# Rescheduling the prologue of a fused cosine-attention and MLP-mixer kernel: token MLPs spread one per slot, norms a slot ahead

## The chip, the cores and the metric

The kernel runs on one core of one Trainium2 chip. The metric is the device time of one execution in microseconds (us). Before the change it was 411.51 us, the median of 3 runs (410.36 to 411.86).

## The reference, cut to what matters

```python
# q, k, v: (8, 12, 448, 64) f32; w_tok1 (448, 256), w_tok2 (256, 448), w_ch1 (768, 1536), w_ch2 (1536, 768)
q_n, k_n = q / (norm(q) + 1e-6), k / (norm(k) + 1e-6)
attn = softmax(q_n @ k_n.T / tau)                    # tau = 0.1
x = (attn @ v) laid out as (8, 448, 768)
u = x + (relu(x.T @ w_tok1) @ w_tok2).T              # token MLP
out = u + relu(u @ w_ch1) @ w_ch2                    # channel MLP
```

## The kernel before

Work goes by pairs of heads: 8 batches of 6 pairs, 48 in all. A loop pass is called a *slot* here; slot `i` does the scores of pair `i`, the product with v of pair `i - 1`, and older pairs' token MLPs. The channel MLP is cut into units (one group of matmuls each) that wait in a list and are fed into the slots as filler for TensorE.

The helpers that the argument touches:

```python
def load_qk(i):                       # q and k of a pair, 224 KB each, on SyncE's DMA queue
    ...
    nc.sync.dma_start(out=st[nm][:]..., in_=src[b, h0:h0 + 2]...)
def square(i, a, act=False):          # squares of q or k: GpSimd, or ScalarE with act=True
def sums(i): nc.vector.tensor_reduce(...)            # row sums of the squares, VectorE
def norms(...):                       # 1/norm from the sums: ScalarE (and VectorE with dve=True)
def scale(i, a): (eng or nc.gpsimd).tensor_tensor(...)   # q, k times 1/norm, GpSimd
def cast_v(i): nc.gpsimd.tensor_copy(...)            # v to f16
def tpose(i): ...                     # q, k transposed by TensorE (pairs below 12), by DMA after
def tok1(i): ...                      # matmul and rectification on VectorE
def tok2(i, pe=False):
    ...
    nc.vector.tensor_tensor(out=u, in0=psU[:], in1=st["x"][:], op=ALU.add)
    if pe:
        return
    nc.sync.dma_start_transpose(out=ut[b][:, pj], in_=u.rearrange("p m d -> p (m d)"))
def upose(i): ...                     # the same transpose by TensorE, with a VectorE copy
def m_ch1(b, ct): ...                 # one channel unit: needs the transposed u of all six pairs
```

The slots of batch 0 (cut):

```python
for i in range(1, NP_ALL + 1):
    b, pj = i // NPAIR, i % NPAIR
    if i < NPAIR:
        toks = {2: [0], 3: [1], 4: [2], 5: [3, 4]}.get(i, [])
        ...                            # scores 0 and 1, sums and norms of pair i + 2 (i < 5)
        for t in toks[:1]: tok1(t)
        pv(i - 1, 0)
        ...
        for t in toks[:1]: tok2(t)     # ends in the DMA transpose of u
        pv(i - 1, 1)
        for t in toks[1:]: tok1(t)
        score(i, 3)
        ...
        for t in toks[1:]: tok2(t)
        if i == 1: place_w2()
        else: weights_ch1(i - 2)       # a quarter of w_ch1 (1.18 MB read) from GpSimd's queue
        load_v(i + 4)
        load_qk(i + 6)
        continue
    ...                                # slot 6: token MLP of pair 5, transposed by TensorE
    # slots 7 to 11: SC_AT, SQ_AT, SU_AT say which pairs are scaled, squared and summed;
    # feed(quota, 1.0) forces one channel unit at each of three places
```

## Time and profile before

| reading | value | view |
|---|---|---|
| TensorE, 90 us to the last matmul at 403.4 us | 100% busy but for 0.1 us | busy time by window |
| slots 2 to 4, 5, 6, 7, 8 to 11 | 14.4, 6.7, 7.0, 8.65, 28.1 us | same, by slot |
| TensorE idle in slots 2 to 11 | 10.9 us | same |
| clock at half | 18.8 to 22.2 and 83.7 to 87.1 us | same |
| DMA, 18 to 50 us | 201 GB/s | same |

Since TensorE has nothing but work from 90 us to its last matmul, all that can be gained lies in the first 90 us and in the 5.4 us after that matmul. The first view is busy time by window, for TensorE alone, with windows cut at the starts of the slots' first scores. The columns are length, TensorE's busy time (and instructions), granted clock (1.00 is full), share of the DMA engines, and GB/s moved. The DMA share adds up the times of packets, which overlap, so it can pass 1.

```profile
core 0: us, PE busy (x), PEclk, DMA share, GB/s
18.86:33.24 14.38, 12.79 (x193) 0.88 1.10 204
33.24:39.94 6.70, 5.00 (x83) 1.00 1.29 219
39.94:46.97 7.03, 4.45 (x70) 1.00 1.30 188
46.97:55.62 8.65, 7.22 (x84) 1.00 1.26 258
55.62:83.72 28.10, 24.49 (x304) 1.00 1.18 235
```

The rows are slots 2 to 4, 5, 6, 7 and 8 to 11. Length less busy time is idleness: 1.7 us in slot 5, 2.6 in slot 6, 1.4 in slot 7, 3.6 in slots 8 to 11. The second view lists what TensorE waited for from 12 to 100 us: engine, tile and line, then what released it, total us, times, longest. PE is TensorE, DVE VectorE, ACT ScalarE, POOL GpSimd, SPq SyncE's queue; L299 is a line of that kernel's file. Of the tiles, psS are scores and pt their exponentials; kq is q and k scaled, pst and qk the same transposed; psO is the product with v and x its result; psR, rt and psU are the token MLP's first product, its rectification and its second product; u is the sum with x, ut its transpose; psG is a channel unit; qf, kf and vf are loaded q, k and v, vt is v cast, sq the squares.

```profile
PE psU L299 <- DVE rt L288: 3.3, 4, 2.3
PE psS L256 <- ACT pt L258: 2.9, 5, 0.8
PE pst L235 <- POOL kq L221: 2.7, 3, 1.2
PE psG L321 <- DMA ut<-u: 1.4, 2, 1.3
```

The first line's 2.3 us falls in slot 11, where a rectification sits on VectorE behind a row sum whose squares GpSimd had not finished. The third view is SyncE's DMA queue as a timeline, which shows the order in which transposes and loads are issued:

```profile
37.69 8.13 SPq L305 DMA_TRANSPOSE ut<-u  x2
45.91 0.53 SPq L110 DMA_DIRECT2D vf<-in_v_dram  x1
46.54 0.41 SPq L104 DMA_DIRECT2D qf<-in_q_dram  x1
```

The two transposes are those of u of pairs 3 and 4. Both go out ahead of the loads of pairs 9 to 13, since both token MLPs are in slot 5.

### The profile page before, as it was taken

How to read it: one execution, taken by the hardware profiler on the slowest of the kernel's cores; microseconds unless marked ns; L12 is line 12 of the kernel's file. 1: busy time of each engine (PE TensorE's matmuls, PEld its weight loads, DVE VectorE, ACT ScalarE, POOL GpSimd, SP SyncE). 2: the span in 40 equal slices, each digit the busy share in tenths (PEclk: the TensorE clock that was granted, in tenths of full speed). 3: DMA queues.
4: the chain of work that ended last, by engine and by line, in shares of the span. 5: the costliest groups of instructions: out<-in, count | busy, mean ns of one | idle time of the engine just before them, and what ended most of it. 6: DMA issues, size and time to landing. Idle time of an engine off the chain costs nothing.

```text
span 408.8 us, 10066 instructions
## 1 busy us (share of the span) xinstructions
PE 386.9 (95%) x4120; PEld 237.9 (58%) x4120; DVE 205.5 (50%) x439; ACT 240.4 (59%) x388; POOL 218.8 (54%) x257
## 2 busy tenths in 40 slices
PE   6888699789999999999999999999999999999994
PEld 5566466456655666566565665656656566655562
DVE  5777656554636556455454556445545434312022
ACT  5987688844686536864687447783587544521400
POOL 7895599884839191858558570949173800000000
PEclk9899999989999999999999999999999999999999
DMA  8999999974867787666979588767755543103022
GB/s 208 268 188 213 195 288 218 230 192 121 215 149 167 154 221 176 167 146 169 191 143 203 132 223 173 167 173 162 206 122 104 113 104 78 27 19 111 0 79 78
DMA packets 103680, 64.34 MB, mean 157 GB/s; under 512 B 62417, under 2 KB 100049, under 8 KB 103633
## 3 DMA queue, kind: packets, MB, share of 16 engines
q1 hardware_dynamic: 98016, 58.48, 62.6%
q0 software_dynamic: 5616, 5.21, 8.3%
q8 instruction: 32, 0.52, 0.6%
q14 instruction: 16, 0.12, 0.1%
HBM read 43.45 MB, written 11.01 MB: 133 GB/s over the span
## 4 chain that ended last, share of the span: by engine, by line
PE 89%; DVE 4%; DMA 3%; issue 1%; ACT 1%; POOL 1%; DVEq 0%; SPq 0%
PE psF L336 27%; PE psG L321 27%; PE psO L272 12%; PE psS L256 11%; PE psU L299 5%; PE psR L285 5%; DMA ut<-u 2%; DVE ssq L198 1%; PE pst L235 1%; DMA kf<-in_k_dram 1%; PE warm L249 1%; DVE rt L288 1%; POOL sq L187 0%; ACT sq L185 0%; DVE qk L237 0%
## 5 line engine op out<-in xcount | busy, mean ns | idle before, releaser
L258 ACT ACTIVATE pt<-psS 112x896 f16<-112x896 f32 x192 | 166.0, 915 | 83.9 <-PE psS L256 83.5
L321 PE MATMUL psG<-ut,wc1t 128*128 128x448 f16 x576 | 123.0, 353 | 1.4 <-DMA ut<-u 1.4
L336 PE MATMUL psF<-wc2t,gt 128*128 128x384 f16 x672 | 116.9, 327 | 0.0
L221 POOL TENSOR_TENSOR kq<-kf,rn 112x512 f16<-112x512 f32 x47 | 50.1, 1065 | 102.0 <-ACT rn L213 82.5
L336 PEld LDWEIGHTS <-gt 128*128 128x128 f16 x672 | 63.2, 98 | 43.6 <-issue 5.5
L324 ACT ACTIVATE gt<-psG 128x448 f16<-128x448 f32 x96 | 51.9, 545 | 55.1 <-PE psG L321 55.1
L340 DVE TENSOR_TENSOR ost<-psF,u 128x384 f32<-128x384 f32 (+1 forms) x64 | 35.7, 557 | 94.9 <-PE psF L336 92.8
L321 PEld LDWEIGHTS <-wc1t 128*128 128x128 f16 x576 | 51.2, 98 | 49.3 <-issue 11.6
L198 DVE TENSOR_REDUCE ssq<-sq 112x16 f32<-112x1024 f32 (+1 forms) x49 | 58.2, 1189 | 9.7 <-ACT sq L185 6.5
L272 PEld LDWEIGHTS <-pt 112*128 112x128 f16 x1536 | 53.0, 99 | 16.2 <-ACT gt L324 7.0
L256 PE MATMUL psS<-qk 64*128 64x448 f16 x384 | 56.2, 362 | 4.1 <-ACT pt L258 2.9
L272 PE MATMUL psO<-vt,pt 112*128 112x65 f16 x1536 | 59.1, 195 | 0.0
L187 POOL TENSOR_TENSOR sq<-kf 112x512 f32<-112x512 f32 x46 | 47.8, 1039 | 4.4 <-DMA kf<-in_k_dram 2.3
L302 DVE TENSOR_TENSOR u<-psU,x 128x512 f16<-128x512 f32 x48 | 33.0, 687 | 31.3 <-PE psU L299 31.2
L221 POOL TENSOR_TENSOR kq<-qf,rn 112x512 f16<-112x512 f32 x45 | 46.9, 1043 | 0.0
L288 DVE TENSOR_SCALAR rt<-psR 128x256 f16<-128x256 f32 x48 | 20.2, 421 | 47.5 <-PE psR L285 47.4
L276 DVE TENSOR_TENSOR x<-psO,rec 128x256 f16<-128x256 f32 x96 | 40.8, 425 | 3.3
L187 POOL TENSOR_TENSOR sq<-qf 112x512 f32<-112x512 f32 x39 | 40.6, 1040 | 0.0
L299 PE MATMUL psU<-rt,w2t 128*128 128x128 f16 x384 | 29.3, 219 | 3.5 <-DVE rt L288 3.3
L299 PEld LDWEIGHTS <-w2t 128*128 128x128 f16 x384 | 25.3, 98 | 12.0 <-issue 5.5
L285 PE MATMUL psR<-x,w1t 128*128 128x128 f16 x384 | 29.8, 221 | 0.8 <-DVE x L276 0.8
L285 PEld LDWEIGHTS <-w1t 128*128 128x128 f16 x384 | 25.3, 99 | 8.9 <-issue 1.2
(40 smaller groups left out, 148.9 us busy)
## 6 DMA issues: line engine op xcount, KB each, us to landing
qf<-in_q_dram SPq DMA_DIRECT2D x48, 224.0 KB, 3.8
kf<-in_k_dram SPq DMA_DIRECT2D x48, 224.0 KB, 3.6
vf<-in_v_dram SPq DMA_DIRECT2D x48, 224.0 KB, 3.1
out_dram<-ost SPq DMA_DIRECT2D x8, 336.0 KB, 3.0
wc1t<-in_moe_w_ch_dram POOLq DMA_DIRECT2D x4, 576.0 KB, 10.8
wc2t<-in_moe_w_ch_dram POOLq DMA_DIRECT2D x2, 1152.0 KB, 16.4
out_dram<-ost SPq DMA_DIRECT2D x8, 288.0 KB, 3.1
out_dram<-ost SPq DMA_DIRECT2D x8, 240.0 KB, 2.9
```

What stands on the lines that cost most here:

```text
L187: nc.gpsimd.tensor_mul(out=pipe[i]["sq"][:, a], in0=src, in1=src)
L198: nc.vector.tensor_reduce(out=half[i // HP]["ssq"][:, a0:a1, lo:lo + 2 * NCH], in_=pipe[i]["sq"][:, a0:a1], axis=AXX.X, op=ALU.add)
L221: (eng or nc.gpsimd).tensor_tensor(out=st["kqn"][:, a].rearrange("p c g e -> p g c e"), in0=side(i, a), in1=_bcast_free(rn, E), op=ALU.mult)
L256: nc.tensor.matmul(psS[:, hh, 0:S], qk[hb:hb + 64, c * SC:c * SC + 128], qk[hb:hb + 64, S:2 * S], start=True, stop=True)
L258: nc.scalar.activation(out=pts[i % 2][:, 2 * S * c:2 * S * (c + 1)].rearrange("p (h s) -> p h s", h=2), in_=psS[0:SC, :, 0:S], func=AF.Exp ...
L272: nc.tensor.matmul(psO[:, m, 0:E + 1], pts[i % 2][:, at:at + 128], vt[:, g, c, 0:E + 1], start=(c == 0), stop=(c == NCH - 1))
L276: nc.vector.tensor_tensor(out=st["x"][:, :, hh * E:(hh + 1) * E], in0=psO[:, :, 0:E], in1=_bcast_free(rec[:], E), op=ALU.mult)
L285: nc.tensor.matmul(psR[:, tt], w1t[:, w1[m], tt * 128:(tt + 1) * 128], st["x"][:, m], start=(m == 0), stop=(m == 3))
L299: nc.tensor.matmul(psU[:, m], w2t[:, tt, lo:lo + 128], st["rt"][:, tt], start=(tt == 0), stop=(tt == TT - 1))
L321: nc.tensor.matmul(psG[:], wc1t[:, dt, ct * 128:(ct + 1) * 128], ut[b][:, dt].rearrange("p m s -> p (m s)")[:, lo:lo + S], start=(dt == 0) ...
L324: nc.scalar.activation(out=gt[:, ct, (b % 2) * S:(b % 2 + 1) * S], in_=psG[:], func=AF.Relu)
L336: nc.tensor.matmul(psF[:], gt[:, ct, lo:lo + 128], wc2t[:, ct, dh * DH:(dh + 1) * DH], start=(ct == 0), stop=(ct == CT - 1))
```

## The change

The intent: one token MLP per slot, two pairs behind the scores, so that slot 5 does not hold two (slot 6 then holds those of pairs 4 and 5); row sums at the head of a slot, of squares made a slot earlier, so that VectorE never blocks on GpSimd; channel units no longer forced three to a slot in slots 7 to 11, so that slot 11 keeps some; 18 warming matmuls in slot 1 to hold the clock; and, in the last batch, the rows shared by two batches first, so that the kernel ends on a plain group. The diff, cut to its core:

```diff
-                for m in range(3 + b % 2) for dh in range(NDH)]
+                for m in ((3, 0, 1, 2) if b == B - 1 else range(3 + b % 2)) for dh in range(NDH)]
-    SC_AT = {6: [7], 7: [8], 8: [9], 9: [10], 10: [11, 12], 11: [13]}
-    SQ_AT = {6: [8], 7: [9], 8: [10, 11], 9: [12, 13], 10: [14], 11: [15, 16]}
-    SU_AT = {6: [8], 7: [9], 8: [10], 9: [11, 12], 10: [13, 14], 11: [15]}
+    SC_AT = {7: [8], 8: [9], 9: [10], 10: [11, 12], 11: [13]}
+    SQ_AT = {7: [10], 8: [11, 12], 9: [13], 10: [14, 15], 11: [16]}
+    SU_AT = {7: [9], 8: [10], 9: [11, 12], 10: [13], 11: [14, 15]}
@@ slots 1 to 5
-                toks = {2: [0], 3: [1], 4: [2], 5: [3, 4]}.get(i, [])
-                if i < 5:
-                    sums(i + 2)
-                    norms(i + 2, i + 3)
-                for t in toks[:1]:
-                    tok1(t)
+                sums(i + 2)
+                norms(i + 2, i + 3)
+                if i >= 2:
+                    tok1(i - 2)
                 pv(i - 1, 0)
...
+                if i == 1:
+                    warm(10)
                 tpose(i + 1)
                 score(i, 2)
-                for t in toks[:1]:
-                    tok2(t)
+                if i >= 2:
+                    tok2(i - 2)
                 pv(i - 1, 1)
...             (8 more warming matmuls after score(i, 3) of slot 1)
@@ slot 6
+                tok1(i - 2)
                 pv(i - 1, 0)
...
+                squares(9)
                 tpose(i + 1)
+                pv(i - 1, 1)
+                score(i, 2)
+                tok2(i - 2)
                 tok1(i - 1)
-                score(i, 2)
+                score(i, 3)
                 tok2(i - 1, pe=True)
@@ slots 7 and later
+            least = 0.0 if early else 1.0
...
+                    for t in SU_AT[i]:
+                        sums(t)        # now ahead of scaling and squaring; norms likewise
-            feed(quota * 0.28, 1.0)
+            feed(quota * 0.28, least)
```

In slot 6 the loads of pairs 12, 13 (q, k) and 10 (v) stand early in both kernels. So pair 4's `tok2`, now in slot 6, issues its transpose of u after them and after the loads at the end of slot 5.

More of the change, by code (lines that the diff above doesn't have):

```diff
@@ L454 @@
                 score(i, 1)
-                if i == 5:
-                    square(7, 1, act=True)
-                    square(7, 0)
-                if i < 5:
-                    sums(i + 2)
-                    norms(i + 2, i + 3)
-                for t in toks[:1]:
-                    tok1(t)
+                sums(i + 2)
+                norms(i + 2, i + 3)
+                if i >= 2:
+                    tok1(i - 2)
                 pv(i - 1, 0)
-                if i < 5:
-                    norms(i + 2, i + 3, dve=True)
+                norms(i + 2, i + 3, dve=True)
                 cast_v(i)
-                if i < 4:
-                    square(i + 3, 0)
+                square(i + 3, 0)
+                if i == 1:
+                    warm(10)
                 tpose(i + 1)
                 score(i, 2)
-                for t in toks[:1]:
-                    tok2(t)
+                if i >= 2:
+                    tok2(i - 2)
                 pv(i - 1, 1)
-                for t in toks[1:]:
-                    tok1(t)
                 score(i, 3)
-                if i < 4:
-                    square(i + 3, 1, act=True)
-                if i == 5:
-                    sums(7)
-                    norms(7, 8)
-                    norms(7, 8, dve=True)
-                for t in toks[1:]:
-                    tok2(t)
+                if i == 1:
+                    warm(8)
+                square(i + 3, 1, act=True)
                 if i == 1:
@@ L491 @@
                 continue
+            if i == NPAIR:
+                load_qk(12)
             if i + 7 < NP_ALL:
-                load_qk(i + 7 if i > NPAIR else 12)
-            if i == NPAIR:
-                load_qk(13)
+                load_qk(i + 7)
             if i == 8:
@@ L501 @@
                 score(i, 1)
-                square(8, 1, act=True)
-                square(8, 0)
+                sums(8)
+                norms(8, 9)
+                tok1(i - 2)
                 pv(i - 1, 0)
-                pv(i - 1, 1)
+                norms(8, 9, dve=True)
                 cast_v(i)
                 load_v(i + 4)
+                squares(9)
                 tpose(i + 1)
+                pv(i - 1, 1)
+                score(i, 2)
+                tok2(i - 2)
                 tok1(i - 1)
-                score(i, 2)
+                score(i, 3)
                 tok2(i - 1, pe=True)
-                score(i, 3)
-                sums(8)
-                norms(8, 9)
-                norms(8, 9, dve=True)
-                upose(i - 1)
+                continue
+            if i == NPAIR + 1:
                 queue += ch1_units(b - 1)
-                continue
             early = i < 12
+            least = 0.0 if early else 1.0
             if pj == 0:
@@ L526 @@
                 score(i, 1)
+                if i == NPAIR + 1:
+                    upose(i - 2)
                 if early:
+                    for t in SU_AT[i]:
+                        sums(t)
+                    for n in sorted({t // HP for t in SU_AT[i]}):
+                        ts = [t for t in SU_AT[i] if t // HP == n]
+                        norms(ts[0], ts[-1] + 1, act=True)
                     for t in SC_AT[i]:
@@ L554 @@
                 score(i, 3)
-            if early:
-                for t in SU_AT[i]:
-                    sums(t)
-                for n in sorted({t // HP for t in SU_AT[i]}):
-                    ts = [t for t in SU_AT[i] if t // HP == n]
-                    norms(ts[0], ts[-1] + 1, act=True)
-            feed(quota * 0.25, 1.0)
+            feed(quota * 0.25, least)
             tok1(i - 1)
-            feed(quota * 0.25, 1.0)
+            feed(quota * 0.25, least)
             tok2(i - 1)
```

## The prediction

> **What bounds it now.** Busy time by window: TensorE is 100% busy from 90 us to the last matmul at 403.4 us, so nothing is gained there. Loss lies in the prologue (pairs 1 to 11). TensorE idles 10.9 us from 18.9 to 83.7 us and 1.8 us just before. Its granted clock falls to 0.50 twice, each time after idling: 19.0 to 22.2 us and 83.8 to 87.0 us; half of 2 x 3.25 us is lost. That is in line with the Trainium skill, "TensorE: Matmul & The Clock Gate", "What's actually happening" (half rate after idling, about 3.4 us to recover). So about 16 us are at stake.
>
> Slots, from the starts of their first scores in the timeline: 2 to 4 take 4.6 us, paced by ScalarE (four exponentials of 0.92 us, a square of 0.63, norms 0.5); slot 5 7.3, slot 6 7.0 (idle 1.7 and 2.6), 7 8.65 (1.4 idle, mostly waiting for the transposed u), 8 to 10 6.9 to 7.6, 11 6.6 with 3.1 idle: its rectification sits behind a VectorE row sum that waits for GpSimd squares (79.5 to 81.6 us); this 2.3 us wait is the longest.
>
> **What changes.** Same work, plus 18 warming matmuls (12 took 1 to 1.4 us) in idle time of slot 1.
> - Warming: slot 2 runs at full clock, 1.2 us saved (then ScalarE paces it), 0.2 paid.
> - Pair 4's token MLP leaves slot 5 for 6: slot 5 becomes like 4, 4.6 us (-2.7); slot 6 about 5.2 (-1.8), though it holds two token MLPs and a serial chain matmul, rectify, matmul, add.
> - Channel units, three per slot in 7 to 10 and none in 11, become two per slot in 7 to 11; two (2 x 1.14 us) are deferred to slot 12. Sums come at the slot's head, of squares made a slot earlier, so the 2.3 us wait and the second clock dip should go (1.6 us).
> - GpSimd becomes the co-limit: a square or scale takes 1.0 us net, a cast 0.6, weight issues about 2. Counted from scaling pair 7, it has cast pair 10 some 31 us later, pair 11 at 36 us (now 42, with waits). TensorE needs the former at about that time: small waits in slots 10 and 11, and ScalarE (two norm groups) stretches slots 9 and 11. I expect 25 us for slots 8 to 11 (now 28.1).
> - Slot 7: pair 4's transposed u is made later, behind three pairs of loads: a wait of 1 to 3 us, slot about 8 us (-0.65).
> - Last batch's rest rows first: the last group ends in one 0.56 us addition instead of two, but its first store starts as before: 0.1 us, perhaps 0.5.
>
> Sum: 1.0 + 2.7 + 1.8 + 0.65 + 3.1 - 2.3 + 1.6 + 0.1 = 8.6 us; I take off half a microsecond for collisions. Essentially all is on the critical path, since TensorE never idles afterwards.
>
> **Prediction:** 403.4 us, range 400.3 to 407.3. Faster by over 2% 0.47, within 2% 0.51, slower 0.02.
>
> **Right or wrong in the profile.** Clock 1.0 from 19 to 22 us; slot 5 near 4.6 us; score of pair 12 starting near 74.5 us instead of 83.7; no wait over 1 us for a rectification in slot 11; no half-clock stretch near 75 us; TensorE's idle total in slots 2 to 11 down from 10.9 to about 5 us.
>
> **What would make it wrong.** Loads: the same bytes (240 GB/s mean in 19 to 84 us) in less time may make squares or the transposed u late, with a long idle in slot 7 and a new clock dip. GpSimd's casts late in slots 10 and 11 would do the same (405 to 407). If all waits vanish, 400.

## The result, and the profile after

The changed kernel took 413.56 us (median of 4 runs, 413.21 to 413.96) against 411.62 us for the kernel before in the same rounds (410.36 to 411.86). The ratio is 1.0054, with a 95% interval of 1.0031 to 1.0076. A ratio here and below is the mean time of one kernel's fast runs over the mean of the other's from the same rounds, so it is not quite the ratio of the quoted medians.

Busy time by window, TensorE, the kernel after, again slots 2 to 4, 5, 6, 7 and 8 to 11:

```profile
18.93:32.25 13.32, 11.75 (x192) 1.00 1.10 212
32.25:36.85 4.60, 3.90 (x66) 1.00 1.23 229
36.85:43.71 6.86, 5.04 (x82) 1.00 1.39 162
43.71:61.63 17.92, 8.16 (x82) 0.71 1.18 255
61.63:85.81 24.18, 22.77 (x300) 1.00 1.12 212
```

Slots 2 to 5 and 8 to 11 became shorter, about as predicted. Slot 6 hardly changed. Slot 7 grew from 8.65 to 17.92 us, and its clock averaged 0.71. TensorE's waits from 12 to 100 us in the kernel after say why:

```profile
PE psG L321 <- DMA ut<-u: 9.5, 2, 5.7
PE psR L285 <- DVE x L276: 2.3, 3, 0.9
PE psS L256 <- ACT pt L258: 2.1, 4, 0.7
```

The wait for the rectification in slot 11 is gone, as intended. In its place the first channel unit waits 9.5 us for the transposed u: 3.8 us for pair 3's and 5.7 us for pair 4's. The chain of waits, in order of time (start, us, what), runs through that second wait:

```profile
40.62 10.51 DMA vf<-in_v_dram
51.13 0.02 issue
51.14 0.02 SPq L305
51.16 0.03 issue
51.19 5.37 DMA ut<-u
56.56 0.04 issue
56.60 0.91 PE psG L321 x2
```

Pair 4's transpose could not be issued until the load of v of pair 9, issued eight places earlier in the queue, had landed after 10.5 us. (In the compiled program eight completion counters take turns in this queue. In none of the 17 traces does one of its DMAs start before the DMA eight places ahead has landed.) Then it took another 5.4 us. SyncE's queue in the kernel after:

```profile
37.46 3.07 SPq L305 DMA_TRANSPOSE ut<-u  x1
40.62 0.82 SPq L110 DMA_DIRECT2D vf<-in_v_dram  x1
...
50.38 0.31 SPq L110 DMA_DIRECT2D vf<-in_v_dram  x1
51.19 1.19 SPq L305 DMA_TRANSPOSE ut<-u  x1
```

Pair 3's transpose was issued at 37.46 us, much as before (37.69), and landed near 50.3 us in both kernels. TensorE now wants it at 46.5 us instead of 49.2.

In terms of slots, after minus before: slot 5 starts 1.0 us earlier; slot 5 -2.1; slot 6 -0.2; slot 7 +9.3; slots 8 to 11 -3.9; two deferred units +2.3; the half-clock stretch at 84 us is gone, -1.6; the tail after the last matmul -0.3 (5.1 us against 5.4). That sums to +2.5 us, and the two profiled spans differ by 2.6 us (411.4 and 408.8).

### The profile page after: what moved, and what is told of

It is laid out like the page before. It is cut to its first block, busy times and chain, and to the rows that moved or that the text cites. A ratio compares the mean times of both kernels' runs of the same rounds, so it can differ in the third digit from the quotient of the medians.

```text
span 411.4 us, 10104 instructions
## 1 busy us (share of the span) xinstructions
PE 386.8 (94%) x4138; PEld 237.7 (58%) x4138; DVE 205.1 (50%) x439; ACT 241.1 (59%) x392; POOL 218.8 (53%) x257
## 4 chain that ended last, share of the span: by engine, by line
PE 86%; DVE 6%; DMA 5%; ACT 1%; issue 1%; POOL 0%; SPq 0%; DVEq 0%
PE psF L336 27%; PE psG L321 26%; PE psO L272 11%; PE psS L256 10%; PE psU L299 5%; PE psR L285 5%; DMA vf<-in_v_dram 3%; DVE ssq L198 2%; DMA ut<-u 1%; PE pst L235 1%; DMA kf<-in_k_dram 1%; ACT sq L185 1%; PE warm L249 1%; DVE x L276 1%; DVE u L302 0%
## 5 line engine op out<-in xcount | busy, mean ns | idle before, releaser
L321 PEld LDWEIGHTS <-wc1t 128*128 128x128 f16 x576 | 51.4, 98 | 56.6 <-issue 18.4
L272 PEld LDWEIGHTS <-pt 112*128 112x128 f16 x1536 | 52.1, 97 | 15.2 <-ACT gt L324 7.0
L272 PE MATMUL psO<-vt,pt 112*128 112x65 f16 x1536 | 58.0, 193 | 0.0
## 6 DMA issues: line engine op xcount, KB each, us to landing
wc1t<-in_moe_w_ch_dram POOLq DMA_DIRECT2D x4, 576.0 KB, 10.9
```

Of the source, the lines that this page charges most:

```text
L272: nc.tensor.matmul(psO[:, m, 0:E + 1], pts[i % 2][:, at:at + 128], vt[:, g, c, 0:E + 1], start=(c == 0), stop=(c == NCH - 1))
L321: nc.tensor.matmul(psG[:], wc1t[:, dt, ct * 128:(ct + 1) * 128], ut[b][:, dt].rearrange("p m s -> p (m s)")[:, lo:lo + S], start=(dt == 0) ...
```

## The experiments

Theory A: the order of the DMA queue alone is at fault, since pair 4's transpose now stands behind the loads of v 9, q and k 11 to 13 and v 10 (the "five loads" of the texts below, eight DMAs). Theory B: the DMA engines carry a backlog, so a faster TensorE meets late data whatever the order. Theory C concerns the clock: the half-clock stretch after the wait costs 1.6 us of its own. Theory D came up on the way: the DMA transposes take transfer rate from everything else. Fifteen runs were made (e9 is the kernel of e6 again). Kernels are compared only within the same rounds.

| run | what | time us (median) | ratio to before, 95% interval |
|---|---|---|---|
| e1 | fill the wait with warming matmuls | 413.1 | 1.0067 (1.0008 to 1.0126) |
| e2 | loads behind pair 4's transpose | 409.1 | 0.9950 (0.9906 to 0.9995) |
| e3 | pairs 3, 4 transposed by TensorE | 409.87 | 0.9982 (0.9921 to 1.0043) |
| e4 | weights later | 413.37 | 1.0051 (0.9997 to 1.0105) |
| e5 | half of w_ch1 not loaded (wrong result) | 406.87 | 0.9906 (0.9856 to 0.9955) |
| e6 | all of batch 0 transposed by TensorE | 403.08 | 0.9824 (0.9774 to 0.9873) |
| e7 | pair 4's token MLP back in slot 5 | 410.91 | 0.9981 (0.9944 to 1.0018) |
| e8 | before, with warming and last rows first | 411.53 | 1.0003 (0.9971 to 1.0036) |
| e9 | as e6, more rounds | 403.14 | 0.9803 (0.9770 to 0.9837) |
| e10 | e9 and dummy DMA transposes | 412.12 | 1.0013 (0.9964 to 1.0062) |
| e11 | e9 and dummy DMA copies | 409.12 | 0.9942 (0.9893 to 0.9991) |
| e12 | before, batch 0 transposed by TensorE | 411.56 | 1.0012 (0.9966 to 1.0058) |
| e13 | e10, loads first | 415.05 | 1.0074 (1.0016 to 1.0132) |
| e14 | e11, loads first | 407.33 | 0.9884 (0.9827 to 0.9941) |
| e15 | after, loads first | 423.77 | 1.0291 (1.0230 to 1.0353) |

### e1: does the half clock matter?

```diff
+            if i == NPAIR + 1:
+                pipe.pop("warm")
+                warm(150)
             feed(quota * 0.28, least)
```

> The changed kernel with 150 warming matmuls (about 8.3 us at full clock) queued just before its first channel unit, inside the wait for pair 4's transposed u. Theory C (the half-clock stretch after the wait costs 1.6 us by itself): the clock stays at 1.0 from 48 to 60 us, the wait for the transposed u still ends near 56.6 us, and the time falls by 1.2 to 1.7 us to about 412. Rival (the matmuls after the wait are paced by something else, so their clock does not matter): no change, 413.5.

The clock was held. Busy time by window of the kernel after, then of e1:

```profile
51.00:59.00 8.00, 2.40 (x14) 0.50 1.14 291
```

```profile
51.00:59.00 8.00, 5.15 (x77) 1.00 1.18 252
```

Yet the time stayed: 413.1 us. In the profiled run the transposed u arrived later (the wait ended at 57.98 us, not 56.60), which ate most of the 1.6 us. Theory C's forecast missed; the rival had the time, though not this reason. The clock dip is real but inside slot 7 its price is not shown to be separable from the arrival of the data.

### e2: order of the queue

The loads of slots 5 and 6 (v 9 and 10, q and k 11 to 13) move to just behind pair 4's `tok2`.

```diff
                 tok2(i - 2)
+                load_v(9)
+                load_qk(11)
+                load_qk(12)
+                load_qk(13)
+                load_v(10)
                 tok1(i - 1)
```

> The changed kernel with the loads of slots 5 and 6 (v 9, q and k 11 to 13, v 10) issued after pair 4's transposed u instead of before it. Theory A (place in the queue): pair 4's transpose lands with pair 3's near 50.5 us, the 5.7 us wait is gone, a wait of about 3.8 us for pair 3's stays, the clock dip goes or shrinks, and the time is 404 to 406. Theory B (the DMA engines are backlogged whatever the order): waits of 8 us or more remain in slot 7 or turn up as waits for squares, time 410 to 413.

Theory A's detail came true: pair 4's transpose arrived 0.5 us after pair 3's (51.60 and 51.07 us), and the 5.7 us wait went. The waits of the channel unit fell to this line of TensorE's waits in e2:

```profile
PE psG L321 <- DMA ut<-u: 4.5, 2, 4.3
```

Only 4.5 us of about 10 came back (413.6 to 409.1 us), less than A forecast. The 4.3 us for pair 3's transpose stayed, and with it a clock dip (0.50 from 52 to 54 us).

### e3: no DMA transpose for pairs 3 and 4

```diff
-                    tok2(i - 2)
+                    tok2(i - 2, pe=i == 5)
...             (slot 6: tok2(4, pe=True), upose(3); slot 7: upose(4) beside upose(5))
```

> The changed kernel with u of pairs 3 and 4 transposed by TensorE, as pair 5's already is, so that no channel unit of slot 7 waits for a DMA. Theory A (only the wait for the transposed u is at fault): no wait in slot 7, the rest as predicted, 400 to 402. Theory B (backlogged DMA engines): the loads of k 9 and k 10 land no earlier than now (about 40.8 and 49.8 us), their squares and row sums hold VectorE in slots 7 and 8, and 2 to 5 us of new waits appear on TensorE: 403 to 406.

No channel unit waited for a DMA any more, but the time only fell to 409.87 us. TensorE's waits in e3, from 12 to 110 us:

```profile
PE psO L272 <- POOL vt L176: 4.3, 3, 1.8
PE psS L256 <- DMA qk<-kq: 2.6, 1, 2.6
PE pst L235 <- POOL kq L221: 1.5, 3, 0.6
```

These are casts and scales that came late because GpSimd's squares of pair 10 started at 50.11 us, when k of pair 10 had landed (49.79 in the kernel after). So B was right that the loads were late too. Its forecast (403 to 406 us) was about 4 us too hopeful even at its upper end.

### e4 and e5: fewer bytes

In e4 the last two quarters of w_ch1 move to slots 7 and 8 and w_ch2 to slot 9.

```diff
-                else:
+                elif i < 4:
                     weights_ch1(i - 2)
...
+            if i in (7, 8):
+                weights_ch1(i - 5)
+            if i == 9:
                 weights_ch2()
```

> The changed kernel, queue order as it is, with the last two quarters of the first channel weight loaded in slots 7 and 8 instead of 4 and 5, and the second channel weight from slot 9. Theory B: with these bytes out of 31 to 50 us the backlog goes; pair 3's transpose takes under 7 us instead of 12.9, the waits in slot 7 sum to under 3 us, and the time is 401 to 404. Theory A: pair 4's transpose stays behind five loads and the DMA eight places before it, the wait shrinks by less than half, 408 to 412.

The run missed its aim: GpSimd ran ahead and issued the two quarters at 41.3 and 46.7 us, in the middle of the wait. But the loads ahead of them did come early, as GpSimd's waits from 30 to 60 us in e4 show (6.3 us for this line in the kernel after):

```profile
POOL sq L187 <- DMA kf<-in_k_dram: 0.3, 1, 0.3
```

Pair 3's transpose, issued at 37.35 us, landed after 5.5 us instead of 12.9, as B forecast. Pair 4's was issued at 45.2 us instead of 51.2, and still landed at 56.0 us, with the late weights under way. So a place in the queue was not enough for it either. The time, 413.37 us, fits neither forecast. In e5 the bytes are really gone. Its output is wrong, which doesn't matter for the time.

```diff
-                else:
+                elif i < 4:
                     weights_ch1(i - 2)
...
-wc1t[:, dt, ct * 128:(ct + 1) * 128]
+wc1t[:, dt, ct % 6 * 128:(ct % 6 + 1) * 128]
```

> Wrong result on purpose: the changed kernel without the last two quarters of the first channel weight (the channel units reuse the first two), so 2.36 MB of reads less between 31 and 50 us, queue order unchanged. Theory B (the DMA engines carry more than they can by 50 us): k 10 lands by 44 us, the waits for the transposed u sum to under 3 us, no half-clock stretch, time 400 to 403. Theory A (only the place of pair 4's transpose behind five loads): the wait falls by less than half, time above 408. The late-weights run already moved k 10 to before 44.2 us, but its weights came back into the wait.

The waits for the transposed u fell from 9.5 to 2.1 us and the time to 406.87 us (405.3 to 408.5). That is between the two forecasts and rules A out as the whole story, since the order was the changed kernel's. The Trainium skill ("DMA: Bandwidth & Descriptors", "Issuing engines are not separate DMA queues") says that DMAs from all issuing engines run on the same 16 DMA engines and interleave. This run agrees: with 2.36 MB of weights gone from GpSimd's queue, the transposes of pairs 3 and 4 on SyncE's landed at 43.0 and 50.4 us instead of 50.3 and 56.6.

### e6 and e9: all of batch 0 transposed by TensorE

```diff
-                    tok2(i - 2)
+                    tok2(i - 2, pe=True)
...             (upose of each pair one slot after its tok2; pairs 4 and 5 in slot 7)
```

> The changed kernel with u of all six pairs of batch 0 transposed by TensorE. DMA traffic fell to about 80 to 140 GB/s in the windows in which a transposed u was under way (24 to 26 and 38 to 42 us), against 200 to 265 around them. Theory D (the transposes themselves take DMA time, about 2 to 4 us each, from the loads): k 10 lands by 45 us instead of 49.8, the casts and squares are not late, TensorE's waits in slots 7 to 12 sum to under 4 us, time 402 to 405. Rival (transposes cost the loads little): as the run that took out only pairs 3 and 4, k 10 at about 50 us, waits of 8 us, 408 to 410.

> The same kernel as the run with all of batch 0 transposed by TensorE, for a firmer interval and as the base of the next two: 403 us, ratio 0.978 to 0.985.

Both gave 403.1 us, against 411.1 and 410.9 us for the kernel before: faster, while the intervals leave open whether by 2%. (One run of e6's four was at 406.81, the profiled one, whose clock is at half from 23.5 to 30.3 us; e9's six lie within 402.93 to 403.95, and its clock is full from 10.6 to 399.7 us.) The wait of slot 7 is gone without loads being late. TensorE's waits in e9 from 43 to 62 us, all of them:

```profile
PE psR L285 <- DVE x L276: 1.8, 2, 1.2
PE psU L299 <- DVE rt L288: 0.2, 1, 0.2
```

Slots 6, 7 and 8 to 11 in e9, and then the stretch from 18 to 50 us:

```profile
38.17:45.46 7.29, 5.41 (x85) 1.00 1.21 250
45.46:51.81 6.35, 6.35 (x86) 1.00 1.14 274
51.81:75.99 24.18, 22.77 (x299) 1.00 1.19 222
18.00:50.00 32.00, 27.33 (x437) 1.00 1.19 253
```

Slots 8 to 11 last 24.18 us, to the hundredth as in the kernel after. Slot 7 takes 6.35 us instead of 17.92. The last line is the new fact: 253 GB/s. The kernel after moved less in the same stretch, at a DMA share no lower:

```profile
18.00:50.00 32.00, 24.18 (x391) 1.00 1.22 205
```

### e7 and e8: parts of the change

In e7 pair 4's token MLP returns to slot 5; the rest of the change stays. In e8 the kernel before gets the 18 warming matmuls and the new order of the last rows, nothing else.

> The changed kernel with pair 4's token MLP put back into slot 5 as before (two in slot 5, one in slot 6), the rest of the change kept. Theory A: pair 4's transpose is again issued before the loads of pairs 9 to 13, both transposes land near 50.5 us as before the change, the wait in slot 7 falls from 9.5 to 1 to 4 us, time 405 to 409. Theory B alone: the first channel unit comes about as late, the waits in slot 7 stay 6 us or more, time 411 to 413.

> The kernel before with the 18 warming matmuls of slot 1 and the last batch's rest rows first, nothing else. Clock theory: clock 1.0 from 19 to 22 us and 1.2 us saved there if what follows is not paced by the DMA engines; tail 0.1 to 0.5 us: ratio about 0.996. Theory B: the 1.2 us is lost again in slot 7 waiting for the transposed u (its wait grows from 1.4 to about 2.6 us): ratio 0.999 to 1.0.

e7 took 410.91 us. The wait for the transposed u fell to 0.4 us, more than A asked for, but GpSimd then waited 6.9 us for k, and 2.7 us of waiting for x, 2.2 us for a transposed q and k and 1.7 us for a cast took its place on TensorE. The loss moved; it did not go. e8 came out at 1.0003: the clock was 1.0 from 19 to 22 us, and the profiled run waited 2.2 us for the transposed u where the kernel before waited 1.4. That is what B forecast, though a difference of a few tenths of a per cent is inside the interval.

### e10, e11, e13, e14: what a transpose costs when nobody waits for it

e10 is e9 with the five DMA transposes of pairs 0 to 4 issued all the same, into a scratch tile that nothing reads. e11 issues plain copies of the same 128 KB instead.

```diff
         if pe:
+            if i < 5:
+                nc.sync.dma_start_transpose(out=junk[:, i], in_=u.rearrange("p m d -> p (m d)"))   # e10
+                nc.sync.dma_start(out=junk[:, i], in_=u)                                            # e11
             return
```

> The previous kernel (all of batch 0 by TensorE) with the five DMA transposes of u of pairs 0 to 4 issued all the same, at their old place in the queue, into a scratch tile that nothing reads. Theory D (a DMA transpose takes time of the DMA engines and of the queue from the loads, whoever waits for it): k 10 lands near 50 us again, squares and casts wait for loads, 407 to 411. Rival (what cost time was only TensorE's wait for the result): 403.

> As the previous one, but the five DMAs are plain copies of the same 128 KB of u into the scratch tile, at the same place in the queue, so they wait for the same u and hold up the loads behind them in the same way, without transposing. If the transposing itself is what costs DMA time: 403 to 404.5, loads early. If what costs is that the loads stand in the queue behind a DMA that waits for u: as the dummy transposes, 407 to 411.

e10 lost 9 us again (412.12 us) although no instruction reads the result. Its new waits are all for loads: GpSimd's squares for k, then TensorE for the cast of v behind them. TensorE, then GpSimd (18 to 80 us), in e10:

```profile
PE psO L272 <- POOL vt L176: 6.5, 3, 4.9
POOL sq L187 <- DMA kf<-in_k_dram: 9.4, 3, 4.9
```

e11 lost 6 us (409.12 us), inside its second forecast: a plain copy also makes the loads behind it wait until u exists. To take that away, e13 and e14 issue the loads of slots 2 to 5 ahead of the dummy of the slot:

```diff
                 if i >= 2:
+                    load_v(i + 4)
+                    load_qk(i + 6)
                     tok2(i - 2, pe=True)
...
-                load_v(i + 4)
-                load_qk(i + 6)
+                if i == 1:
+                    load_v(i + 4)
+                    load_qk(i + 6)
```

> The run with dummy transposes, with the loads of slots 2 to 5 issued before that slot's transpose instead of behind it, so that no load stands behind a DMA that still waits for u. From 18 to 50 us the DMA engines moved 253 GB/s without transposes, 210 with dummy transposes and 228 with dummy copies. If the transposing itself costs (engine time): the rate stays under 225 GB/s, casts and squares stay late, 408 to 412. If the standing behind u costs: rate over 240, 403 to 405. If both, about a third and two thirds as transposes against copies suggest: 405 to 407.

> The run with dummy copies, with the same move of the loads to the front. Standing behind u is all that a plain copy of 128 KB costs: rate back to 245 GB/s or more, 403 to 404.5. Rival (five more DMAs in the queue cost by their number or bytes): 406 to 409.

Busy time by window from 18 to 50 us, in the order e10, e11, e13, e14:

```profile
18.00:50.00 32.00, 26.73 (x429) 1.00 1.25 210
18.00:50.00 32.00, 27.32 (x439) 1.00 1.12 228
18.00:50.00 32.00, 27.34 (x435) 1.00 1.24 221
18.00:50.00 32.00, 27.35 (x435) 1.00 1.19 252
```

With loads first, dummy copies leave the rate at 252 GB/s and dummy transposes hold it to 221. An estimate from these two lines: (252 - 221) GB/s times 32 us is 1.0 MB not moved, or 3.9 us at 252 GB/s, for the four dummies that start before 50 us in e13 (the fifth starts at 50.07 us). Up to 50 us, then, transposes cost more than copies at the same place.

The rate counts the dummies' own bytes, though. In e14 four copies (0.52 MB) land before 50 us, so its loads moved at no more than about 236 GB/s, against 253 in e9. And the times follow less neatly. e13 took 415.05 us (412.7 to 416.4), more than any of its forecasts and no less than e10. e14 took 407.33 us (404.8 to 408.5): not the 403 to 404.5 of its first forecast but the 406 to 409 of its rival, by which five more DMAs cost by their number or bytes. In its profiled run k of pair 15, issued at 54.45 us, lands at 70.93 us (in e9 54.95 and 66.59). A cast then waits behind its squares, TensorE waits 3.7 us for the cast, and the clock is at half from 72.2 to 79.0 us. The copies' 0.66 MB are, by estimate, 2.6 us at 252 GB/s, so they are part of this delay; the rest is open.

Nor do these runs show that the transposes cost by taking transfer rate, as theory D has it. A rival was not tested: a transpose also holds SyncE longer while it is issued, and nothing behind it in the queue goes out meanwhile. In e13 the five issues take 10.9 us, in e14 2.4 us. Pair 3's dummy, in e13 and in e14:

```profile
39.83 4.59 SPq L305 DMA_TRANSPOSE junk<-u  x1
```

```profile
38.57 0.47 SPq L305 DMA_DIRECT2D junk<-u  x1
```

The Trainium skill ("DMA: Bandwidth & Descriptors", "Latency and other measured facts") gives a DMA transpose an effective rate of 261 GB/s where the middle dimension is not contiguous, and about 350 to 400 GB/s in the contiguous case. No run here isolates one, but among loads it does not act like 128 KB of ordinary traffic.

### e12: is the schedule worth anything?

The kernel before, with `tok2(t, pe=True)` and `upose` for all six pairs of batch 0, and nothing else.

> The kernel before, with u of all six pairs of batch 0 transposed by TensorE and nothing else changed. If the change's schedule is worth what I predicted once the DMA engines are relieved, this one keeps the waits of slots 5, 6 and 11 and their clock dip and gains only its 1.4 us wait and little else: 408.5 to 410.5, ratio 0.995 to 1.0. Rival (the relief alone explains the whole gain of the previous ones and the schedule adds nothing): 403 to 405.

411.56 us, about 1 us above the forecast. Its slot 11 still waits 2.3 us for the rectification. So taking the transposes off the DMA queue alone gains nothing, the schedule alone loses 2 us, and the two together gain 8 us.

### e15: the changed kernel with loads first

> The changed kernel itself (real DMA transposes) with the loads of slots 2 to 5 issued before that slot's transpose. If order alone could save it: the wait in slot 7 falls below 3 us and the time to 403 to 406. If transposing costs engine time and pair 4's transpose still comes behind the loads of pairs 9 to 13: the wait stays 5 us or more, 409 to 413.

423.77 us, worse than either forecast. The longest wait for a transposed u grew from 5.7 to 12.9 us, 19.5 us in all:

```profile
PE psG L321 <- DMA ut<-u: 19.5, 3, 12.9
```

A transpose that TensorE waits for must not go behind loads. Nor did loads first help where nobody waits for it (e13, 415.05 us, against e10, 412.12 us).

## Why the prediction was wrong

The forecast was 403.4 us and the result 413.56 us, outside the range.

- **Where it failed.** The step is "Slot 7: pair 4's transposed u is made later, behind three pairs of loads: a wait of 1 to 3 us, slot about 8 us (-0.65)". The waits came to 9.5 us (5.7 for pair 4's u, 3.8 for pair 3's) and the slot to 17.92 us. The cause was named, also under "what would make it wrong", but sized at a third at most. The prediction shows no working for its 1 to 3 us. Half of all transposes in the trace before landed within 3.0 us, but in the stretch in question (30 to 56 us) that trace already showed 6.9 to 12.8 us. And only pair 4's transpose was priced. Pair 3's lands near 50.3 us whatever TensorE does, so every microsecond saved in slots 2 to 6 became a wait. e2 shows this part (4.3 us of waiting), and e2 against the kernel after shows the queue order's part (the 5.7 us wait gone, 4.5 us of time).
- **Shown beneath it.** By 50 us less had been moved with transposes among the loads: 205 GB/s with them, 253 without. e6 and e9 remove the transposes and land at 403.1 us, within the predicted range; e10 puts them back without a reader and loses it all again. Two thirds of that loss (6 of 9 us) come with plain copies too (e11). So it is shown that these DMAs, in this queue and this stretch, cost the gain. How the cost divides into the order of the queue, the bytes, the issue on SyncE and the transposing itself is not shown.
- **Partly luck.** That e9 lands so near 403.4 us does not confirm each step: its slot 6 took 7.29 us where 5.2 was predicted, and its slot 7 took 6.35 us where about 8 was. The two errors largely cancel.
- **Slot 6** was predicted at 5.2 us and took 6.86 (7.29 in e9, with TensorE's own transposes). The term was -1.8 us and measured -0.2. With the second token MLP the slot's TensorE work grew from 4.45 to 5.04 us, and its idle time shrank only from 2.6 to 1.8 us.
- **Slot 5** was right in its end (4.60 us) and about half a microsecond too large in its start: 7.3 us was read, 6.7 is what the first scores give. **Slots 8 to 11** were predicted at 25 us and took 24.18, with the 2.3 us wait and the second clock dip gone. The two deferred units are booked above at the forecast 2.3 us; only their sum with the vanished clock dip is measured (the stretch from slot 12 to the last matmul grew by 0.8 us).
- **Clock.** Slot 2 ran at full clock and slot 5 began 1.0 us earlier, as predicted. But a new dip appeared after the slot 7 wait, which the prediction had listed as a risk. The Trainium skill ("TensorE: Matmul & The Clock Gate", "What's actually happening") describes half rate after an idle window and recovery after about 3.4 us of work. The trace agrees: the clock is at 0.50 from 49.8 us, 3.3 us after TensorE began to wait, to 60.0 us, 3.4 us after the matmuls resumed at 56.6 us.
- **Last rows first.** 0.3 us by the profiled tails; predicted 0.1, perhaps 0.5.

Without the slot 7 and slot 6 errors the sum of the prediction is right within half a microsecond. What was wrong was to treat "the loads may be late" as a tail risk. The same bytes in less time needed more than the 201 GB/s that the kernel before moved from 18 to 50 us.

## What to carry to other kernels

When a prologue is shortened, first divide the bytes that must arrive by the new deadline by the rate that the same stretch sustains; if that fails, the time saved on the engines comes back as a wait. Look for DMAs that only move data on the chip, transposes above all, in a stretch where loads are the limit: here TensorE did them for little (slot 6 took 7.29 us in e9 against 6.86). A result that a DMA carries should be issued ahead of prefetches; moving its producer one slot later can put it behind all of them.

## What the Trainium skill lacked or had wrong

- "DMA: Bandwidth & Descriptors" ("Rules for kernel authors") says that a transpose next to ordinary DMAs needs nothing, which there is about correct results. The page does not say what a transpose costs the loads around it: 221 GB/s with dummy transposes against 252 GB/s with plain copies of the same size, same order, from 18 to 50 us.
- No page says that a DMA may be held at issue until the one eight places earlier in the same queue has landed, as in this compiled program: pair 4's transpose waited for a load issued at 40.62 us that landed at 51.13 us.
- "DMA: Bandwidth & Descriptors" ("Anatomy of one DMA — SWDGE (gpsimd) path") gives about 2 us as the fixed cost of a DMA issued from GpSimd. It gives no time to land in a full queue: here a 224 KB load of v on SyncE's queue took 10.5 us to land, and a transpose 12.9 us.
- "TensorE: Matmul & The Clock Gate" agrees with the trace on half clock after idling. What it cannot tell is when holding the clock pays: 150 filler matmuls held it at 1.0 and the kernel was no faster (413.1 us).
